# First MoE's last outputs placed among the second MoE's slots, and other places for the second pair's operands

## The chip, the cores and the metric

The kernel runs on one core of a Trainium2 chip. The metric is the device time of one execution in microseconds. Before the change the median of three runs is 922.1 us (922.1, 922.1 and 923.27).

## The reference, cut to what matters

```python
# q, k, v: 4 batches, 8 heads, 576 positions, head size 64
q_s = softmax(q, axis=-1); k_s = softmax(k, axis=2)
kv  = einsum('bhsd,bhse->bhde', k_s, v)
x   = einsum('bhsd,bhde->bhse', q_s, kv)      # as 2304 tokens x 512
# first MoE, d_ff 1536
x = ((x @ w_a) * (x @ w_b)) @ w_out
# second MoE, d_ff 2048
h = x @ w_in
P = a0 + a1*h + a2*h**2 + a3*h**3
Q = 1 + |b0|*|h| + |b1|*h**2
out = (P / (Q + 1e-6)) @ w_out2
```

## The kernel before, in words

Every matmul operand of the two MoEs is split in two float32r halves, a high and a low one, and each product is three matmuls: high x high, high x low, low x high (`mm3`, L446 to L449, and L637 to L639 in `mult`). XH and XL hold the halves of the 2304 tokens of the layer's input, as four chunks of 128 features. The tokens are cut into blocks: blocks 0 to 3 are 512 wide and block 4, the narrow one, is 256 wide. ACC holds the sums of the outputs.

**Order of the work.** The kernel writes down every instruction with an engine, an estimated duration, a rank and its reads and writes (class Plan, L35). `Plan.run` (L65) then plays the program through: of all instructions whose inputs are there it takes the one that can start first, and among equals the one of lower rank. The order that comes out is the order in each engine's queue; the chip keeps it, whatever its own durations are. So ranks and duration estimates decide only the order. DMAs are all issued on SP's queue.

**First MoE.** `step1` (L469) handles one filter group f (128 of the 1536 hidden features) for one block n: the a projection into one PSUM bank, a copy of it by ScalarE (L475), the b projection into a second bank, their product on VectorE (L478), its high half on ScalarE (L481) and low half on VectorE (L482). The output products of the step, `rest` (L485), come after the projections of the next step, and go to the banks Y, four of them. After three filters the four banks are added to ACC (L465, or copied there by L463 the first time). There are four filter groups of three, and 60 steps (n1); in the first three groups the block order is 0, 1, 2, 4, 3, in the last one 0 to 4. The last group of the narrow block is done apart by `last_narrow` (L500): bank 4 holds the a projection in its left and the b projection in its right half, so that each filter's copy (L518), product (L519) and split (L523, L524) stand in a chain with the projections; then come the output products, the addition to ACC (L538) and the split of the result into XH and XL (L540, L541). Its ranks are LAST = 60.3 and on.

**Second MoE.** Its input projection is a Strassen-Winograd form: two 512-wide blocks of tokens, two halves of the features and two filters are treated as 2 x 2 blocks, with 7 products in place of 8. `operands` (L549) makes the seven token operands of one pair of blocks from ACC: `less` (L567) subtracts in ACC, `split` writes the high half by ScalarE (L560) and the low one by POOL (L562) or VectorE (L564). Each operand lies in a place of XH and XL, `place(c, b, r)`: chunks 2c + r, block b, so it overwrites tokens that are not read any more. Pair 0 is blocks 0 and 1, pair 1 blocks 2 and 3, and both pairs use the same seven places (`spots`, L791).

A slot (L648) is one pair of filters j for one pair of blocks: seven operands of the weights are loaded from DRAM (they were put there during the first MoE by the `spill` functions), seven products of six matmuls run through the banks ba, be, bb, bc, with copies and additions between banks (L658, L660, L663, L665), and `value` (L587) works out P/Q of each of the four banks in place: five instructions on ScalarE (L593 to L595, L601, L602), one on POOL (L596) and five on VectorE (L597, L598, L603, L605, L607). With `extra`, the filters of the narrow block are projected too, from the same weights, in a fifth bank. There are 16 slots: 8 for pair 0, all with `extra`, then 8 for pair 1. After every second slot `jobs` (L695) issues the output products of a group of four filters: `whole` (L611) splits the value (ScalarE L619, POOL L620), and each 128 tokens are 4 x 3 matmuls into banks 0 and 1 and an addition to ACC.

Buffers are handed out in rings (class Ring, L234): r_op for the weights' operands, r_w2 for the output weights, r_o for the splits of values, r_free and r_seed for PSUM banks. They reuse places of the first MoE's weights and splits (wa, fa).

## Time and profile before

| what | before |
|---|---|
| median of three runs | 922.1 us |
| the profiled execution's own time | 919.76 us |
| its span, first to last instruction | 917.7 us |
| mean granted clock of TensorE | 0.996 |
| busy: TensorE / VectorE / ScalarE / POOL | 893.9 / 647.5 / 554.1 / 408.9 us |

The profile lists for each engine the busy time, and for idle time what ended it. A matmul's record is longer than its pace, since matmuls are pipelined: the pace is read from the starts. PE is TensorE, PEld its weight loads, DVE VectorE, ACT ScalarE, SP the DMA queue. PEclk is the granted clock as a share of full speed. A wait "PE ps L449 <- POOL wa L620" is idle time of TensorE ahead of a matmul of line 449, ended by an instruction of POOL of line 620. The attention and the first MoE go together until 137 us; the second MoE's first product starts at 513.85 us.

### The profile page before, as it was taken

How to read it: one execution, taken by the hardware profiler on the slowest of the kernel's cores; microseconds unless marked ns; L12 is line 12 of the kernel's file. 1: busy time of each engine (PE TensorE's matmuls, PEld its weight loads, DVE VectorE, ACT ScalarE, POOL GpSimd, SP SyncE). 2: the span in 40 equal slices, each digit the busy share in tenths (PEclk: the TensorE clock that was granted, in tenths of full speed). 3: DMA queues.
4: the chain of work that ended last, by engine and by line, in shares of the span. 5: the costliest groups of instructions: out<-in, count | busy, mean ns of one | idle time of the engine just before them, and what ended most of it. 6: DMA issues, size and time to landing. Idle time of an engine off the chain costs nothing.

```text
span 917.7 us, 13161 instructions
## 1 busy us (share of the span) xinstructions
PE 893.9 (97%) x4577; PEld 737.3 (80%) x4577; DVE 647.5 (71%) x1051; ACT 554.1 (60%) x1046; POOL 408.9 (45%) x369
## 2 busy tenths in 40 slices
PE   7999999999999999999989898999999899999998
PEld 6677778888898888988878777888888688888886
DVE  5799642366666866676784479667879978678883
ACT  5978562454444444444442479888687777887771
POOL 4553320235542354535461145636356764455552
PEclk9999999999999999999999999999999899999999
DMA  7655510236664367645431443152433346363422
GB/s 268 192 196 161 181 30 1 91 116 208 220 216 139 117 221 231 206 141 186 142 112 46 149 150 114 57 185 81 151 126 93 135 141 229 96 194 83 157 69 92
DMA packets 60034, 131.23 MB, mean 143 GB/s; under 512 B 6464, under 2 KB 14656, under 8 KB 59968
## 3 DMA queue, kind: packets, MB, share of 16 engines
q1 hardware_dynamic: 59680, 130.39, 44.3%
q8 instruction: 36, 0.59, 0.3%
q14 instruction: 30, 0.25, 0.1%
q10 hardware_dynamic: 288, 0.00, 0.0%
HBM read 100.49 MB, written 29.88 MB: 142 GB/s over the span
## 4 chain that ended last, share of the span: by engine, by line
PE 89%; DVE 5%; ACT 3%; POOL 2%; issue 1%; DMA 1%; ACTq 0%; POOLq 0%; DVEq 0%
PE ps L447 23%; PE ps L449 23%; PE ps L448 23%; PE ps L637 5%; PE ps L639 5%; PE ps L638 5%; PE ps L428 2%; PE ps L402 1%; PE ps L418 1%; DVE ACC L567 1%; DMA coef<-in_moe_b 1%; DVE ACC L465 1%; PE ps L369 1%; DVE fa L280 0%; POOL fa L319 0%
## 5 line engine op out<-in xcount | busy, mean ns | idle before, releaser
L447 PE MATMUL ps<-wa 128*128 128x512 f32 (+1 forms) x528 | 203.9, 386 | 3.4 <-ACT wa L481 1.4
L449 PE MATMUL ps<-wa 128*128 128x512 f32 (+1 forms) x528 | 201.7, 382 | 3.9 <-POOL wa L620 3.9
L448 PE MATMUL ps<-wa 128*128 128x512 f32 (+1 forms) x528 | 201.6, 382 | 1.0 <-DVE wa L482 1.0
L447 PE MATMUL ps<-XH,wa 128*128 128x512 f32 (+1 forms) x528 | 195.5, 370 | 2.7 <-DVE ps L519 1.1
L449 PE MATMUL ps<-XH,wa 128*128 128x512 f32 (+1 forms) x528 | 190.5, 361 | 0.2 <-POOL wa L290 0.2
L448 PE MATMUL ps<-XL,wa 128*128 128x512 f32 (+1 forms) x528 | 190.4, 361 | 0.0
L596 POOL TENSOR_TENSOR fa<-fa 128x512 f32<-128x512 f32 x72 | 93.8, 1307 | 128.2 <-ACT fa L594 117.4
L620 POOL TENSOR_TENSOR wa<-fa,wa 128x512 fp32r<-128x512 f32 x72 | 93.2, 1311 | 61.7 <-ACT wa L619 48.1
L447 PEld LDWEIGHTS ps<-wa 128*128 128x128 f32 x528 | 99.6, 189 | 25.1 <-ACT wa L619 2.0
L449 PEld LDWEIGHTS ps<-wa 128*128 128x128 f32 x528 | 99.7, 189 | 24.4 <-POOL wa L620 5.5
L447 PEld LDWEIGHTS ps<-XH,wa 128*128 128x128 f32 x528 | 99.7, 189 | 20.2 <-ACT wa L523 1.4
L448 PEld LDWEIGHTS ps<-wa 128*128 128x128 f32 x528 | 99.8, 189 | 20.0 <-DVE wa L482 1.8
L290 POOL TENSOR_TENSOR wa<-fa,wa 128x512 fp32r<-128x512 f32 x36 | 50.3, 1403 | 139.5 <-ACT wa L289 135.2
L449 PEld LDWEIGHTS ps<-XH,wa 128*128 128x128 f32 x528 | 99.6, 189 | 15.9 <-POOL wa L290 0.7
L448 PEld LDWEIGHTS ps<-XL,wa 128*128 128x128 f32 x528 | 99.8, 189 | 14.6
L307 POOL TENSOR_TENSOR fa<-fa 128x256 fp32r<-128x256 f32 x96 | 76.2, 817 | 68.9 <-ACT fa L306 65.9
L465 DVE TENSOR_TENSOR ACC<-ps,ACC 128x512 f32<-128x512 f32 (+1 forms) x110 | 72.2, 670 | 36.1 <-PE ps L449 35.9
L478 DVE TENSOR_TENSOR ps<-ps,fa 128x512 f32<-128x512 f32 (+1 forms) x57 | 37.4, 656 | 84.4 <-PE ps L449 84.2
L481 ACT ACTIVATE wa<-ps 128x512 fp32r<-128x512 f32 (+1 forms) x57 | 32.0, 564 | 88.9 <-DVE ps L478 88.9
L603 DVE SCALAR_TENSOR_TENSOR fa<-fa,coef,ps 128x512 f32<-128x512 f32 x72 | 52.9, 743 | 28.7 <-ACT ps L602 28.4
L279 ACT ACTIVATE fa<-fa 128x512 f32<-128x512 f32 x68 | 45.7, 680 | 30.9 <-DVE fa L277 30.3
L597 DVE TENSOR_TENSOR fa<-fa,ps 128x512 f32<-128x512 f32 x72 | 49.1, 683 | 21.3 <-ACT fa L595 21.1
(113 smaller groups left out, 1652.3 us busy)
## 6 DMA issues: line engine op xcount, KB each, us to landing
wi<-fa SPq DMA_DIRECT2D x64, 256.0 KB, 3.9
wa<-wo SPq DMA_DIRECT2D x32, 512.0 KB, 4.4
wa<-wi SPq DMA_DIRECT2D x60, 256.0 KB, 3.0
fa<-in_moe_w_out SPq DMA_DIRECT2D x28, 512.0 KB, 4.2
fa<-in_moe_w_in SPq DMA_DIRECT2D x16, 512.0 KB, 3.7
wo<-fa SPq DMA_DIRECT2D x32, 256.0 KB, 4.3
XH<-wi SPq DMA_DIRECT2D x30, 256.0 KB, 3.0
XL<-wi SPq DMA_DIRECT2D x30, 256.0 KB, 2.8
```

The costliest lines, as they stand in the source:

```text
L290: pool(W, rank, lambda: nc.gpsimd.tensor_tensor(out=t[:, 1, :], in0=hf, in1=t[:, 0, :].bitcast(F32), op=ALU.subtract), [kr, kw], [kw])
L307: pool(HALF, rank, lambda: nc.gpsimd.tensor_tensor(out=lo, in0=src, in1=hi.bitcast(F32), op=ALU.subtract), [ksrc, kt], [kt])
L447: nc.tensor.matmul(o, lh, rh, start=start, stop=False)
L448: nc.tensor.matmul(o, lh, rl, start=False, stop=False)
L449: nc.tensor.matmul(o, ll, rh, start=False, stop=stop)
L465: dve(n, rank, lambda: nc.vector.tensor_tensor(out=a, in0=ps[bank][:, :n], in1=a, op=ALU.add), [psk(bank), ("accr", o)], [("accr", o)])
L596: pool(n, rank, lambda: G.tensor_tensor(out=w, in0=w, in1=u, op=ALU.mult), [ku, kw], [kw])
L597: dve(n, rank, lambda: V.tensor_tensor(out=z, in0=z, in1=h, op=ALU.mult), [kz, kh], [kz])
L603: dve(n, rank, lambda: V.scalar_tensor_tensor(out=z, in0=z, scalar=coef[:, 0:1], in1=h, op0=ALU.add, op1=ALU.mult), [kz, kh], [kz], ptr=1)
L620: pool(W, rank, lambda: nc.gpsimd.tensor_tensor(out=hl[:, 1, :], in0=z, in1=hl[:, 0, :].bitcast(F32), op=ALU.subtract), [kz, kh], [kh])
L637: T.matmul(ps[bank], wh, xh, start=first, stop=False, skip_group_check=True)
L638: T.matmul(ps[bank], wh, xl, start=False, stop=False, skip_group_check=True)
```

## The change

The narrow block's tokens move out of XH and XL into a tile XN of their own, which begins with 64 unused bytes, and its products' halves start 64 bytes into their buffer as well (SIDE). `last_narrow` goes; in the last filter group the block order is 0, 1, 4, 2, 3, so the narrow block has ordinary steps there. The last three steps (block 3) are only `front`; their output products are `late_jobs`, with ranks among the first two slots. Slots 0 and 1 have no `extra` any more; the two missing ones are done in slots 12 and 13, since pair 1 takes the filters in the order 4 to 7, 0 to 3. The second pair's first operand goes to place (1, 3), the other six each to the place of the operand one earlier. Place (1, 3) held weights before; `wa` has three more buffers and `fa` one. The matmul of L802, which read the negative identity, goes. Ranks, which were written in the calls, come from a table K, and duration estimates of VectorE's instructions with two SBUF inputs (dve3) and of ScalarE (178 in place of 150 after the first MoE) are raised.

```diff
-    NW, NRAW, NHL, NSC = 10, 3, 3, 7
+    NW, NRAW, NHL, NSC, NEW = 10, 3, 3, 7, 3
-    LAST = 60.3
-    LATE, SOON = 0.25, -2.0
+    TURN1, NX, SW0, SW1, OP1 = 4, 2, 2, 3, NF2 // 2 - 1
+    FREE, SEED = (4, 5, 6), (2, 3, 7)
+    K = dict(late=0.004, soon=-2.088, asoon=-2.101, wl=1.191, j0=0.621, j1=1.847, jn=1.96, each=0.208, by=0.383, v1=-0.223, v2=0.25, v3=1.089, v4=0.415, v5=0.458, p1=0.05, px=0.629, op=-0.518, w2=0.507, w2f=1.839, o0=-4.578, o1=-1.102, l0=2.934, l1=2.627, l2=2.373, l3=3.783, last=0.577, nx=-4.91, wn=2.147)
...
-    XH = const.tile([P, NCC, NT], F32R, name="XH")
-    XL = const.tile([P, NCC, NT], F32R, name="XL")
+    NW4 = NT // W * W
+    SIDE = 16
+    XH = const.tile([P, NCC, NW4], F32R, name="XH")
+    XL = const.tile([P, NCC, NW4], F32R, name="XL")
+    XN = const.tile([P, 8 * SIDE + 2 * NCC * (NT - NW4)], F32R, name="XN")
...
+    def dve3(n, rank, fn, reads, writes):
+        plan.add("dve", 150 + n * 1.76, rank, fn, reads, writes, port=True)
...
-            act(w, rank, lambda o=o, px=px: A.activation(XH[:, hp, o:o + w], px[:, 0:w], AF.Copy),
-                [kpx], xk("XH", hp, o, w))
+            for a, e in pieces(o, w):
+                xh = X(0, hp, o + a, e - a)
+                act(e - a, rank, lambda px=px, a=a, e=e, xh=xh: A.activation(xh, px[:, a:e], AF.Copy),
+                    [kpx], xk("XH", hp, o + a, e - a))
...
+    def front(f, n, banks, rank):
...
+        o = SIDE if n == NB - 1 else 0
+        hh, ll = hl[:, 0, o:o + nb], hl[:, 1, o:o + nb]
...
-    def last_narrow(fs, ranks):
...
+    def late_jobs(n, hs, ranks):
+        t0, nb = blocks[n]
+        for m, rank in enumerate(ranks):
+            sl = slice(m * P, (m + 1) * P)
+            bank = m % 2
+            for i, (f, (hh, ll, kh)) in enumerate(hs):
+                w, kw = wtile["o", f]
+                pe(3, nb, rank + 0.01 * i, lambda w=w, sl=sl, bank=bank, hh=hh, ll=ll, i=i: mm3(
+                    ps[bank][:, :nb], w[:, 0, sl], w[:, 1, sl], hh, ll, i == 0, i == len(hs) - 1),
+                    [kw, kh], [psk(bank)], fixed=13)
+            add_acc(NCC * t0 + m * nb, nb, bank, False, rank)
...
+    LASTG = [0, 1, NB - 1, 2, 3]
-             for n in (order if g < NF1 // G1 - 1 else range(NB))]
+             for n in (order if g < NF1 // G1 - 1 else LASTG)]
...
-        if n == NB - 1 and b == NF1:
+        if s >= n1 - G1:
             if f == a:
                 pend()
-                last_narrow(range(a, b), [LAST + 0.1 * i for i in range(b - a)])
                 pend = lambda: None
+            late.append((f, front(f, n, AB if s % 2 == 0 else AT, s)))
...
-    pend()
+    abase[0] = 178
+    late_jobs(NB - 2, late, [n1 + K[f"l{i}"] for i in range(4)])
+    narrow_x(n1 + K["nx"])
...
-    r_op = Ring(wa.cuts([(6 * 2 + i) * W for i in range(2)], OP) + spare + wa.cuts([(7 * 2 + i) * W for i in range(2)], OP))
-    r_w2 = Ring(wt(9, 0, 1, 3, 4))
+    r_op = Ring(wa.cuts([(t * 2 + i) * W for t in (13, 14, 6, 7) for i in range(2)], OP))
+    r_w2 = Ring(wt(0, 1, 3, 4, 9))
...
+    r_o = Ring(ha[2:] + ha[:2], ha[:2] + [((h, l), kh + kl) for (h, kh), (l, kl) in spare])
-    r_free, r_seed = Ring((5, 3, 4)), Ring((6, 7, 2))
+    r_free, r_seed = Ring(FREE), Ring(SEED)
...
-    spots.append(spots[0])
+    spots.append([(1, 3)] + spots[0][:-1])
+    turns = [list(range(NP2)), [(j + TURN1) % NP2 for j in range(NP2)]]
-    operands(0, spots[0], n1 - 3.0, 2)
+    operands(0, spots[0], n1 + K["o0"], SW0)
...
-        extra = js < NP2
-        slot(js, js % NP2, spots[js // NP2], extra)
-        if js == 0:
-            pe(1, W, step2_rank(0, 0.2), lambda: nc.tensor.matmul(ps[2], minus, XH[:, 0, 0:W], start=True, stop=True),
-               xk("XH", 0, 0, W) + [psk(2)], [psk(2)], fixed=13)
-        if js == NP2 - 1:
-            operands(1, spots[1], step2_rank(NP2, -0.5), 3)
+        p, i = divmod(js, NP2)
+        j = turns[p][i]
+        extra = j >= NX if p == 0 else j < NX
+        slot(js, p, j, spots[p], extra)
+        if js == OP1:
+            operands(1, spots[1], step2_rank(NP2, K["o1"]), SW1)
...
-    jobs(2 * (NB // 2) - 1, NF2 // G2 - 1, NS + 0.6, 0.01, (4, 3, 5, 2), 0.6)
+    jobs(2 * (NB // 2) - 1, turns[1][-1] // gp, NS + K["last"], 0.01, False, True, (4, 3, 5, 2), 0.6)
```

## Rows read from the trace of the kernel before

**Rows 1.** The page: busy time, share of the span and instructions of each engine.
```profile
PE 893.9 (97%) x4577; PEld 737.3 (80%) x4577; DVE 647.5 (71%) x1051; ACT 554.1 (60%) x1046; POOL 408.9 (45%) x369
```

**Rows 2.** Windows: stretch, width, busy PE, PEld, DVE, ACT, POOL; clock; DMA share, GB/s.
```profile
137.00:460.00 323.00, 323.00 (x1577) 273.46 (x1576) 203.85 (x349) 138.27 (x271) 127.81 (x142) 1.00 0.50 160
460.00:505.00 45.00, 42.56 (x186) 34.37 (x185) 28.73 (x38) 14.91 (x30) 19.91 (x18) 1.00 0.20 71
505.00:545.00 40.00, 36.83 (x219) 31.86 (x217) 21.35 (x37) 23.54 (x41) 10.61 (x10) 1.00 0.52 162
545.00:570.00 25.00, 21.12 (x98) 16.30 (x98) 22.81 (x36) 22.41 (x38) 12.43 (x10) 1.00 0.33 98
570.00:704.00 134.00, 134.00 (x657) 113.64 (x656) 104.20 (x159) 106.45 (x179) 70.95 (x56) 1.00 0.36 111
704.00:735.00 31.00, 27.74 (x109) 21.23 (x108) 30.33 (x42) 23.87 (x41) 23.76 (x17) 0.89 0.46 154
735.00:880.00 145.00, 145.00 (x642) 120.03 (x641) 114.26 (x173) 114.08 (x192) 72.44 (x58) 1.00 0.45 141
```

**Rows 3.** Waits view, TensorE: total us, times, longest us.
```profile
PE ps L449 <- POOL wa L620: 3.9, 3, 2.6
...
PE ps L447 <- ACT wa L481: 1.4, 1, 1.4
...
PE ps L447 <- DVE ps L519: 1.1, 1, 1.1
...
PE ps L447 <- DVE ACC L538: 0.5, 1, 0.5
```

**Rows 4.** Timeline of TensorE around a wait: start, duration, instruction.
```profile
547.77 0.39 PE L639 MATMUL ps<-XH 128*128 128x512 f32 x1
549.49 0.50 PE L637 MATMUL ps<-XH,XL 128*128 128x512 f32 x1 [1.33 <-DVE ps L663]
549.83 0.39 PE L638 MATMUL ps<-XL 128*128 128x512 f32 x1
```

**Rows 5.** Timeline of TensorE after the longest wait.
```profile
726.47 0.61 PE L449 MATMUL ps<-wa 128*128 128x512 f32 x1 [2.63 <-POOL wa L620]
...
727.30 0.63 PE L448 MATMUL ps<-wa 128*128 128x512 f32 x1
727.72 0.63 PE L449 MATMUL ps<-wa 128*128 128x512 f32 x1
```

**Rows 6.** The page: DMA issues, KB each, median us to landing.
```profile
wa<-wo SPq DMA_DIRECT2D x32, 512.0 KB, 4.4
```

**Rows 7.** Groups by line and form, 570 to 704 us, ScalarE, VectorE, POOL: count, busy, mean ns.
```profile
L594 ACT ACTIVATE fa<-fa,bmag 128x512 f32<-128x512 f32 x25 | 20.1, 817 | 3.8 <-DVE ps L605 3.8
...
L605 DVE SCALAR_TENSOR_TENSOR ps<-fa,qbias,ps 128x512 f32<-128x512 f32 x27 | 20.0, 748 | 0.0
L597 DVE TENSOR_TENSOR fa<-fa,ps 128x512 f32<-128x512 f32 x25 | 17.0, 684 | 4.6 <-ACT fa L595 4.5
L465 DVE TENSOR_TENSOR ACC<-ps,ACC 128x512 f32<-128x512 f32 x16 | 10.9, 689 | 4.9 <-PE ps L449 4.8
...
L596 POOL TENSOR_TENSOR fa<-fa 128x512 f32<-128x512 f32 x25 | 32.3, 1300 | 33.8 <-ACT fa L594 32.7 <-DVE fa L603 1.0
```

**Rows 8.** Groups by line and form, 704 to 735 us, VectorE and POOL.
```profile
L567 DVE TENSOR_TENSOR ACC<-ACC 128x512 f32<-128x512 f32 x8 | 8.7, 1099 | 0.0
...
L562 POOL TENSOR_TENSOR XL<-ACC,XH 128x512 fp32r<-128x512 f32 x8 | 11.0, 1395 | 5.9 <-ACT XH L560 5.9
```

**Rows 9.** The same subtraction in 570 to 704 us.
```profile
L567 DVE TENSOR_TENSOR ACC<-ACC 128x512 f32<-128x512 f32 x1 | 0.7, 684 | 0.0
```

**Rows 10.** The split of attention, 100 to 137 us, ScalarE.
```profile
L431 ACT ACTIVATE XH<-ps 128x288 fp32r<-128x288 f32 x8 | 3.3, 412 | 1.3 <-PE ps L428 0.8
```

**Rows 11.** Timeline of TensorE in a visit to the narrow block.
```profile
259.63 0.28 PE L449 MATMUL ps<-XH,wa 128*128 128x256 f32 x1
259.75 0.28 PE L447 MATMUL ps<-XH,wa 128*128 128x256 f32 x1
```

192 lines of the change are left out of this document (87 added, 105 removed).

## The prediction

> **What bounds the kernel now.** I read the page first. TensorE is busy for 893.9 of the 917.7 us of the span [rows 1], so a change that leaves the products as they are can win only where TensorE stands. Next I read the windows view, cut where TensorE's share falls. From 137 to 460 us, from 570 to 704 and from 735 to 880 TensorE has no idle time at all [rows 2]; VectorE has slack there (114 of 145 us in the last). Between them lie three weak stretches: the end of the first MoE with its narrow block (460 to 545), the first slots of the second MoE (545 to 570), and the change from its first token pair to its second (704 to 735). Their idle is width minus PE: 2.44, 3.17, 3.88 and 3.26 us, together 12.75.
>
> The waits view, from which rows 3 show four, names thirteen waits in these four stretches, from 2.6 us (POOL's low half in L620) down to 0.5 us (the adds of L538) [rows 3]; two lie in 460 to 505, five in 505 to 545, four in 545 to 570, two in 704 to 735. A wait costs more than its idle. In the timeline a dense 512-column matmul starts 0.227 us after the one before; around an idle time of 1.33 us the two starts are 1.72 and 0.34 us apart [rows 4], so 1.60 is lost: 0.27 beyond the idle. Around the wait of 2.63 us the clock falls too: the starts 0.43 us apart [rows 5] are the 1.2 GHz level against 0.227 at 2.4 GHz. From 726.5 to 733.4 us fourteen matmuls go at that pace: 14 x 0.20 = 2.8 us.
>
> The loss that can be won back, by stretch:
> - first MoE's end: 2.44 + 2 x 0.27 = 2.98
> - narrow block: 3.17 + 5 x 0.27 = 4.52
> - first slots: 3.88 + 4 x 0.27 = 4.96
> - change of pair: 3.26 + 2 x 0.27 + 2.8 = 6.60
>
> That is 19.06 us. The profiled execution took 919.76 us, 2.3 under the median of 922.1; I subtract from the median, since none of the terms depends on the offset.
>
> **The narrow block becomes an ordinary step.** Before, L500 runs the last three filters of the narrow block through one bank, in a chain a, copy, b, multiply, split, add; its waits run from 1.1 us for the product of L519 to 0.5 for L538 [rows 3]. After, the block takes the ordinary pairs of banks and stands between blocks 1 and 2, so the next step's projections lie under its chain. The rows for that are 137 to 460, where it is visited as such a step and TensorE is not idle [rows 2]. Ends: 0 and today's 4.52. I take 0.3.
>
> **The last outputs move.** The last three steps (512-wide block 3) become fronts only; their output products, 4 x 3 x 3 = 36 matmuls or 36 x 0.227 = 8.2 us, are issued among slots 0 and 1. So nothing on TensorE waits any more for the L481 and L482 of the last steps, of which L481 gave the 1.4 us in the first stretch [rows 3]. That wait came because VectorE was giving the operands' subtractions (L567) their turns. The subtractions now have rank 55.4 instead of 57 and still stand ahead of the last fronts, but there only the late products wait. Ends: 0 and 2.98. I take 0.5, for block 2's outputs, which still wait for their splits. What the late products hold until then (three split buffers, three weights) is asked for last by the reordered rings, and places 13 to 15 are new; without that cover the first loads would wait some 4.4 us for a landing [rows 6].
>
> **The first slots.** A slot has 42 matmuls, 9.5 us, but four values. A value has five VectorE instructions, 0.684 to 0.748 us, sum 3.6 us [rows 7]; with L663 and L665 at 0.7 a slot asks VectorE for 15.8 us. Until jobs can start, VectorE is the limit. The change moves the extra (narrow) value of slots 0 and 1 to slots 12 and 13 (2 x 3.6 = 7.2 us of VectorE; 735 to 880 has 30 us of slack [rows 2], without which 7.2 would be the price), and gives TensorE 8.2 us of late products where it had 12.9 us of narrow ones. VectorE needs 2 x 15.8 + 4 late additions at 0.69 = 34.4 us for slots 0 and 1, and begins some 5.5 us in (three products and two ScalarE steps, [rows 7]). Slot 2 needs the bank of slot 1's third value, at about 5.5 + 34.4 - 3.6 = 36.3 us; TensorE has work until 9.5 + 8.2 + 9.5 + 4 products (5.4) + narrow extra (2.9) = 35.5. So about 1 us is late, if the late products fall exactly into the gaps; I take 3. The lower end is 0, the upper is worked out below.
>
> **The change of pair.** The second pair's operands are 22 instructions with both inputs in SBUF: on VectorE 8 subtractions and 4 splits, on POOL 10. Here L567 takes 1099 ns and POOL's L562 1395 [rows 8], against 684 for an L567 with POOL free [rows 9]. Before, the first of them overwrites a place that slot 7 still reads, so the whole burst of 12 x 1.1 = 13.2 us on VectorE lands in 700 to 732, where VectorE is busy 30.3 of 31 us [rows 2], and L620 comes late behind POOL's splits. After, the first operand goes to a place that nobody reads any more, and each other one to the place of the product one earlier. Both halves of the first operand and four of the eight subtractions can then run before slot 7: 4 + 1 of 12 VectorE instructions, 5.5 us. The waits to hide are 3.26 us. Ends: 0 and 6.6. I take 2, because the other 17 still crowd one slot.
>
> **Small terms.** The matmul with the negative identity at slot 0 goes: -0.2. A 288-wide split in attention is cut in two for four units: at most one more L431, 0.41 us [rows 10], four times, under a TensorE that is busy; 0, at most 1.6 without cover. Weights are loaded at later ranks on SP's queue, whose DMA share is 0.36 to 0.45 in the slots [rows 2]: 0, at most one landing of 4.4 [rows 6]. The narrow block's own halves (four copies on ScalarE, four subtractions on POOL, 256 wide) are now issued some three steps ahead of slot 0, in 460 to 505, where POOL is busy 19.9 of 45 us and ScalarE 14.9 [rows 2], and first read in slot 2: 0. Larger rings and other cost figures in the planner add no instruction. The second pair's other order of filters is the same work.
>
> **The 64 bytes.** Narrow matmuls start 0.12 us apart [rows 11], 13 ns over their 256 columns at 2.4 GHz; the wide ones, 0.227, are over theirs by the same 13. The trace of before has no shifted one. There are 12 x 2 x 4 x 3 + 12 x 4 x 3 + 8 x 8 x 3 = 624 of them; if the shift took all 13 away it would win 8.0 us; a like loss is not excluded. I take 0, because both widths show the same surplus, so that it does not look like a matter of where the narrow block lies.
>
> The Trainium skill's page "TensorE: Matmul & The Clock Gate" ("Wait — 56ns, not 53.3ns?") gives a warm matmul its columns plus about 2.5 ns; by that the narrow ones could be 10 ns faster, and the sum 6 us lower. The trace does not agree with 2.5 ns for these matmuls.
>
> **Sum.** Left over: 0.3 + 0.5 + 3 + 2 = 5.8. Gain: 19.06 - 5.8 + 0.2 = 13.5. 922.1 - 13.5 = 908.6 us.
>
> **Rivals.**
> *The pair's crowd stays* (chance 0.2): the same 22 instructions still share the port in one slot, so the last stretch keeps 6.6. For it: beside POOL's splits an L567 takes 0.4 us longer [rows 8, 9], and a place alone does not change that. Against it: 5.5 us of burst is released early. Time: 908.6 + 4.6 = 913.2.
>
> The skill's page "SBUF — State Buffer" ("Who interferes with whom") says that of a VectorE instruction with two SBUF inputs and a reading GpSimd one the second blocks fully until the first ends; at 0.684 + 1.3 that would be up to 1.98 us each, 23.8 for the twelve in place of 13.2, and this rival the likelier case. The trace agrees with a contention, but its mean of 1.1 is not a full block.
>
> *Everything hides* (0.12): 1 us left in all. 922.1 - 19.06 + 1 - 0.2 = 903.8.
>
> *The narrow pace improves* (0.05): with the main case 908.6 - 8.0 = 900.6.
>
> *Slots run one after the other* (0.08, the slower side). The place is slots 1 and 2, with three banks of each kind and no jobs yet. If each has to wait for the whole of the one before, TensorE stands 15.8 - 9.5 us plus the latency of one value. That chain is Abs, scale, POOL's product, root, square and two VectorE steps: with at most 0.817 for a ScalarE step, 1.3 for POOL's and 0.7 for VectorE's [rows 7] some 6 to 7 us. So 13 us each, 26 in all, less 8.2 of late products, plus two falls of the clock at 2.8: 23.4 us in place of my 3. Time: 908.6 + 20.4 = 929.0. It decides against the change where the first slots lose over 18 us. Against it: before, with five values a slot, they lost 5.
>
> *Waits only change places* (0.04): losses add up to 19 again, 922.
>
> **How the numbers follow.** Main case 0.51, and 0.2, 0.12, 0.05 on the same side: faster 0.88. A measurement of this kernel tells 0.2%, 1.8 us, from no change: same 0.04. Slower 0.08. The range 900 to 918 takes in the main case with its ends (startup up to 10 us, shift of 8 us), and the first three rivals; left out are the two last.
>
> **What would show it.** Right: the PE windows around the end of the first MoE without idle, no wait on a narrow half; the late products lying singly among slot 0's and 1's; first subtractions of the second pair before slot 7; a clock of 1.00 throughout. Wrong: idle over 5 us in the first 40 us of the slots, POOL's L620 as TensorE's longest wait near the change of pair, or a clock near 0.65 anywhere after 460 us.

## The result, and the profile after

The changed kernel takes 898.93 us (median of four, 898.63 to 899.73) against 922.13 us for the kernel before on the same chip (922.1 to 923.27): ratio 0.9747, 95% interval 0.973 to 0.9764. That is 23.2 us by the medians and 20.8 by the profiled executions (919.76 and 898.94); 13.5 was forecast, and the result lies 1.1 us below the range. The medians of the kernels below are of four to ten executions; one of x1_extra_first took 2067.89 us, its three others 900.83 to 901.56.

The page's busy line answers to [rows 1]: TensorE has lost 8.1 us of busy records and its share has risen from 97 to 99%.

```profile
PE 885.8 (99%) x4576; PEld 734.9 (82%) x4576; DVE 638.1 (71%) x1055; ACT 557.5 (62%) x1050; POOL 404.2 (45%) x369
```

The windows of the changed kernel, with the columns of [rows 2]; the cuts follow its own stretches.

```profile
137.00:460.00 323.00, 323.00 (x1583) 273.06 (x1583) 201.51 (x349) 139.00 (x275) 127.97 (x142) 1.00 0.50 163
460.00:505.00 45.00, 45.00 (x246) 39.14 (x245) 28.33 (x48) 17.84 (x38) 19.71 (x22) 1.00 0.26 84
505.00:520.00 15.00, 15.00 (x68) 12.43 (x67) 5.51 (x8) 7.09 (x12) 2.58 (x2) 1.00 0.64 208
520.00:570.00 50.00, 50.00 (x231) 41.30 (x231) 41.99 (x65) 45.67 (x76) 24.42 (x19) 1.00 0.37 111
570.00:690.00 120.00, 120.00 (x588) 101.61 (x587) 100.94 (x154) 102.69 (x172) 70.42 (x55) 1.00 0.39 122
690.00:735.00 45.00, 45.00 (x200) 37.26 (x199) 39.31 (x61) 35.05 (x59) 27.15 (x22) 1.00 0.50 163
735.00:880.00 145.00, 144.79 (x660) 119.92 (x659) 115.24 (x175) 112.90 (x186) 73.13 (x57) 1.00 0.40 127
```

Busy PE equals the width in every stretch up to 735 us. The four weak stretches of before are full, and the clock, 0.89 around the change of pair before, is 1.00.

TensorE's waits over the whole span of the changed kernel (total us, times, longest us), the three longest of the six that the view lists:

```profile
PE ps L392 <- ACT fa L384: 2.4, 1, 2.4
PE ps L833 <- POOL ident masks.py:199: 1.6, 1, 1.6
PE ps L441 <- POOL ACC L414: 0.9, 2, 0.7
```

All six belong to the start, the attention or the preparation of weights; none lies in one of the four stretches, and no wait of [rows 3] has a successor. To count what that is worth I add up, matmul by matmul, the distance from one start to the next minus the pace of its width, from the first narrow matmul of the second filter group (257.95 us before, 258.48 after) to the last matmul of the kernel, and call the sum the **loss by starts**. Only excesses of over 0.04 us are counted. The stretch shrinks from 655.47 to 634.16 us, so by 21.3. The loss by starts falls from 21.5 to 1.2 us (0.36 of it between 520 and 540 us, 0.75 between 860 and 880); 516 narrow matmuls in that stretch are 1.5 ns faster each, 0.8 us; the matmul with the negative identity was 0.2. 20.3 + 0.8 + 0.2 = 21.3: the account closes. Up to 258 us the changed kernel is 0.5 us later, hence 20.8 for the whole.

The late products, by line and form between 513.5 and 545 us (count, busy us, mean ns, idle before them):

```profile
L474 PE MATMUL ps<-wa 128*128 128x512 f32 x13 | 5.1, 389 | 0.0
```

L475 and L476 have 13 each as well; 36 of the 39 are the late products (the last three belong to the first `jobs`). They lie in packets of 9, 18 and 9, from 522.99, 529.28 and 540.44 us, without idle time: the first two in slot 1, which begins at 521.6, the third in slot 2, which begins at 537.4.

The operands of the second pair, VectorE and POOL, 570 to 690 us, against [rows 8, 9]:

```profile
L579 DVE TENSOR_TENSOR ACC<-ACC 128x512 f32<-128x512 f32 x7 | 4.9, 714 | 0.0
...
L574 POOL TENSOR_TENSOR XL<-ACC,XH 128x512 fp32r<-128x512 f32 x9 | 11.8, 1324 | 6.8 <-ACT XH L572 6.2 <-DVE fa L609 0.7
```

Seven of the eight subtractions are done and nine of POOL's ten splits have begun when the second pair's first slot begins at 690.4 us; the first subtraction starts at 633.95. The subtraction takes 714 ns in the mean, not 1099: six of the seven take 0.68 us and one 0.91.

### The profile page after: what moved, and what is told of

Read it like the earlier page. It is cut to its first block, busy times and chain, and to the rows that moved or that the text cites. A ratio compares the mean times of both kernels' runs of the same rounds, so it can differ in the third digit from the quotient of the medians.

```text
span 897.2 us, 13154 instructions
## 1 busy us (share of the span) xinstructions
PE 885.8 (99%) x4576; PEld 734.9 (82%) x4576; DVE 638.1 (71%) x1055; ACT 557.5 (62%) x1050; POOL 404.2 (45%) x369
## 4 chain that ended last, share of the span: by engine, by line
PE 95%; DVE 2%; ACT 1%; DMA 1%; POOL 0%; issue 0%; ACTq 0%
PE ps L474 25%; PE ps L476 25%; PE ps L475 24%; PE ps L649 6%; PE ps L651 6%; PE ps L650 6%; PE ps L451 2%; PE ps L425 1%; PE ps L441 1%; DMA coef<-in_moe_b 1%; PE ps L392 1%; DVE fa L303 0%; DVE small L411 0%; DVE fa L305 0%; DVE ACC L492 0%
## 5 line engine op out<-in xcount | busy, mean ns | idle before, releaser
L474 PE MATMUL ps<-wa 128*128 128x512 f32 (+1 forms) x520 | 199.5, 384 | 0.2
L476 PE MATMUL ps<-wa 128*128 128x512 f32 (+1 forms) x520 | 197.4, 380 | 0.0
L475 PE MATMUL ps<-wa 128*128 128x512 f32 (+1 forms) x520 | 197.2, 379 | 0.0
L474 PE MATMUL ps<-XH,wa 128*128 128x512 f32 x384 | 154.5, 402 | 0.0
L476 PE MATMUL ps<-XH,wa 128*128 128x512 f32 x384 | 150.0, 391 | 0.2 <-POOL wa L313 0.2
L475 PE MATMUL ps<-XL,wa 128*128 128x512 f32 x384 | 149.6, 390 | 0.0
L474 PEld LDWEIGHTS ps<-wa 128*128 128x128 f32 x520 | 97.6, 188 | 19.9 <-DVE ACC L492 1.4
L476 PEld LDWEIGHTS ps<-wa 128*128 128x128 f32 x520 | 97.6, 188 | 18.8
L313 POOL TENSOR_TENSOR wa<-fa,wa 128x512 fp32r<-128x512 f32 x36 | 50.4, 1406 | 138.9 <-ACT wa L312 130.7
L475 PEld LDWEIGHTS ps<-wa 128*128 128x128 f32 x520 | 97.7, 188 | 18.1
L632 POOL TENSOR_TENSOR wa<-fa,wa 128x512 fp32r<-128x512 f32 x70 | 90.4, 1298 | 40.5 <-ACT wa L631 31.5
L525 ACT ACTIVATE wa<-ps 128x512 fp32r<-128x512 f32 (+1 forms) x60 | 33.3, 554 | 88.9 <-DVE ps L521 88.6
L649 PE MATMUL ps<-XH,wa 128*128 128x512 f32 x224 | 87.4, 390 | 0.0
L651 PE MATMUL ps<-XH,wa 128*128 128x512 f32 x224 | 87.2, 389 | 0.0
L650 PE MATMUL ps<-XL,wa 128*128 128x512 f32 x224 | 87.1, 389 | 0.0
L476 PEld LDWEIGHTS ps<-XH,wa 128*128 128x128 f32 x384 | 72.1, 188 | 16.1 <-POOL wa L313 0.7
L474 PEld LDWEIGHTS ps<-XH,wa 128*128 128x128 f32 x384 | 72.2, 188 | 14.5
L475 PEld LDWEIGHTS ps<-XL,wa 128*128 128x128 f32 x384 | 72.2, 188 | 13.6
```

Of the source, the lines that this page charges most:

```text
L313: pool(W, rank, lambda: nc.gpsimd.tensor_tensor(out=t[:, 1, :], in0=hf, in1=t[:, 0, :].bitcast(F32), op=ALU.subtract), [kr, kw], [kw])
L474: nc.tensor.matmul(o, lh, rh, start=start, stop=False)
L475: nc.tensor.matmul(o, lh, rl, start=False, stop=False)
L476: nc.tensor.matmul(o, ll, rh, start=False, stop=stop)
L632: pool(W, rank, lambda: nc.gpsimd.tensor_tensor(out=hl[1], in0=z, in1=hl[0].bitcast(F32), op=ALU.subtract), [kz, kh], [kh])
L649: T.matmul(ps[bank], wh, xh, start=first, stop=False, skip_group_check=True)
```

## The experiments

Every kernel was compared with the kernel before on the same chip. The sets of runs stand on several chips, where the medians of before differ by 1.6 us, so a difference of 1 or 2 us between two kernels is read from the traces, not from the medians. The last column is the loss by starts of the profiled execution; those of q2, s2 and p1 took 914.35, 909.73 and 909.75 us, more than their medians. No run undoes the larger rings, the other PSUM banks (FREE, SEED), the second pair's other order of filters, or the lower `dynamic_dma_scratch_size`, which the diff sets in `build` and the section on the change does not name.

| kernel | median us | ratio, 95% interval | loss by starts |
|---|---|---|---|
| before | 920.6 to 922.1 | 1 | 21.5 |
| after | 898.93 | 0.9747 (0.973 to 0.9764) | 1.2 |
| s1_old_ranks | 909.65 | 0.9856 (0.9839 to 0.9874) | 10.8 |
| s2_old_costs | 906.2 | 0.983 (0.9806 to 0.9853) | 12.1 |
| s4_old_costs_new_order | 904.76 | 0.9818 (0.9799 to 0.9837) | 8.2 |
| j1_jittered_ranks | 901.92 | 0.9786 (0.9764 to 0.9808) | 4.3 |
| l1_no_late | 905.84 | 0.9834 (0.9817 to 0.985) | 7.8 |
| x1_extra_first | 901.43 | 0.9785 (0.9766 to 0.9805) | 3.6 |
| q2_old_structure_new_order | 910.11 | 0.9887 (0.9861 to 0.9913) | 16.2 |
| p1_same_places | 907.02 | 0.9831 (0.9806 to 0.9856) | 9.2 |
| p2_same_places_new_order | 901.14 | 0.9784 (0.9764 to 0.9805) | 3.7 |
| p3_same_places_new_order2 | 898.22 | 0.975 (0.9734 to 0.9766) | 0.7 |
| n1_narrow_step | 923.34 | 1.0024 (1.0015 to 1.0034) | 24.0 |
| b1_before_new_costs | 927.27 | 1.0063 (1.0048 to 1.0078) | 26.7 |
| h1_no_shift | 900.28 | 0.976 (0.9743 to 0.9777) | 1.3 |
| c3_shift_128 | 900.34 | 0.9771 (0.9755 to 0.9788) | 1.5 |
| c2_pad | 910.32 | 0.9878 (0.9861 to 0.9895) | 2.8 |
| c1_wide_shift | 912.02 | 0.9898 (0.9882 to 0.9915) | 1.2 |
| c5_wide_shift_aligned | 906.81 | 0.9841 (0.9826 to 0.9856) | 1.6 |
| v1_first_ranks | 900.42 | 0.9775 (0.9754 to 0.9795) | 2.3 |

### The order: ranks and estimates

**s1_old_ranks** keeps everything but gives the table K the numbers that the calls of before had (0.5 for the late products, which had none).

```diff
+    K = dict(late=0.25, soon=-2.0, asoon=-2.0, wl=1.0, j0=0.85, j1=1.85, jn=1.85, each=0.25, by=0.5, v1=0.1, v2=0.25, v3=0.3, v4=0.35, v5=0.45, p1=0.05, px=0.4, op=-1.0, w2=0.3, w2f=0.2, o0=-3.0, o1=-0.5, l0=0.5, l1=0.5, l2=0.5, l3=0.5, last=0.6, nx=0.3, wn=0.0)
```

> The changed kernel with the ranks that the kernel before had (late 0.25, soon -2.0, operands at -3.0 and -0.5, jobs at 0.85 and 1.85 and so on; the late products, which had none, at 0.5). Everything else of the change stays. If the structure of the change (late products, narrow block as a step, places) took the waits away, it stays at 898.9 to 902. If the searched order did, the 5.8 us that I had left over for the first slots and the change of pair come back or more: 904 to 910, with idle time of TensorE in the first 40 us of the slots.

It is 10.7 us slower than the changed kernel. The first two lines below are from its waits view, the third from its windows:

```profile
PE ps L474 <- DVE fa L619: 3.4, 1, 3.4
...
PE ps L649 <- ACT ps L670: 1.7, 1, 1.7
```

```profile
520.00:570.00 50.00, 44.55 (x200) 36.76 (x199) 40.08 (x60) 40.41 (x69) 23.72 (x19) 0.97 0.35 106
```

TensorE waits again for VectorE's last step of a value (L619), and 7.6 of 10.8 us of loss lie between 520 and 560 us. The same instructions, in an order that is not fitted to them, lose half of the gain.

**s2_old_costs** takes the raised estimates back, and with them `port=True`, by which the planner lets none of these instructions run beside one of POOL.

```diff
-        plan.add("dve", 150 + n * 1.76, rank, fn, reads, writes, port=True)
+        plan.add("dve", 90 + n * 1.15, rank, fn, reads, writes)
...
-    abase[0] = 178
```

> The changed kernel with the planner's duration estimates of before: 679 ns in place of 1051 for VectorE's instructions with two SBUF inputs, which no longer hold POOL in the plan, and 150 in place of 178 for ScalarE. The ranks are the new ones. If ranks and structure are enough, 898.9 to 901. If the plan has to know these durations, L632 is late again around the change of pair and the time is 902 to 908.

**s4_old_costs_new_order** does the same with ranks found anew, by some thousands of small changes of K, each judged by where the kernel's own planner leaves TensorE without work; all ranks "found anew" below come about in this way.

```diff
+    K = dict(late=-9.209, soon=-12.967, asoon=-11.728, wl=-2.729, j0=2.983, j1=2.244, jn=2.573, each=-1.509, by=0.899, v1=2.133, v2=-1.443, v3=2.52, v4=0.596, v5=-2.691, p1=0.093, px=0.73, op=7.798, w2=6.548, w2f=-10.075, o0=6.788, o1=10.108, l0=2.887, l1=2.859, l2=12.584, l3=11.884, last=4.939, nx=-11.98, wn=-24.827)
```

> The changed kernel with the duration estimates of before and the ranks found anew under them. If a search can make up for wrong durations, 898.5 to 900. If the plan is only as good as its durations, waits stay where VectorE's two-input instructions are many (end of the first MoE, change of pair): 902 to 908.

s2 is 7.3 and s4 5.8 us slower than the changed kernel. Of s4, waits and a window:

```profile
PE ps L475 <- DVE wa L526: 1.9, 3, 0.9
...
PE ps L474 <- ACT wa L525: 1.3, 1, 1.3
```

```profile
460.00:505.00 45.00, 41.83 (x218) 35.75 (x217) 30.49 (x44) 16.60 (x36) 21.66 (x22) 0.96 0.24 83
```

The last steps' halves (L525, L526) are late again: 5.2 us of loss between 460 and 480 us. The timeline of VectorE shows what they wait for:

```profile
463.32 3.55 DVE L579 TENSOR_TENSOR ACC<-ACC 128x512 f32<-128x512 f32 x3
466.80 0.41 DVE L526 TENSOR_TENSOR wa<-ps,wa 128x256 fp32r<-128x256 f32 x1
```

Three of the operands' subtractions take 1.18 us each here and stand in front of the half. The old estimate gives them 90 + 512 x 1.15 = 679 ns, the raised one 150 + 512 x 1.76 = 1051. Without a POOL instruction beside it a subtraction does take 0.68 us (the changed kernel's at 633.95); what the old plan leaves out is the wait for POOL (last section). A search that believes 679 does not take them out of the way, and new ranks win back 1.4 of the 7.3 us, with intervals that overlap. Estimate and port mark were undone together, so the share of each stays open.

**b1_before_new_costs** is the kernel before with the raised estimates and their port mark alone.

```diff
+    def dve3(n, rank, fn, reads, writes):
+        plan.add("dve", 150 + n * 1.76, rank, fn, reads, writes, port=True)
...
+    abase[0] = 178
```

> The kernel before with the changed kernel's duration estimates alone (1051 ns for VectorE's instructions with two SBUF inputs, which hold POOL in the plan, and 178 for ScalarE after the first MoE). If the wrong estimates made the waits at the change of pair and at the end of the first MoE, 6 to 9 us go: 913 to 916. If the structure made them, 920 to 923.

It is slower than before. Window and waits of it:

```profile
735.00:880.00 145.00, 139.23 (x608) 113.31 (x607) 108.95 (x165) 109.71 (x184) 73.19 (x57) 1.00 0.44 140
```

```profile
PE ps L641 <- DVE ps L667: 4.0, 2, 3.2
PE ps L641 <- ACT ps L662: 3.8, 5, 1.1
PE ps L641 <- DVE fa L611: 3.1, 1, 3.1
```

The 3.2 us of loss between 460 and 480 are gone, but a stretch that lost nothing before [rows 2] loses 5.8 us of PE. Under the old ranks the better plan is worth nothing here.

**j1_jittered_ranks** is the control: every rank moved at random by some hundredths.

```diff
+    K = dict(late=0.062, soon=-2.104, asoon=-2.107, wl=1.247, j0=0.593, j1=1.841, jn=1.979, each=0.227, by=0.369, v1=-0.174, v2=0.241, v3=1.125, v4=0.469, v5=0.491, p1=0.087, px=0.571, op=-0.584, w2=0.476, w2f=1.863, o0=-4.503, o1=-1.163, l0=2.949, l1=2.584, l2=2.336, l3=3.769, last=0.612, nx=-4.899, wn=2.206)
```

> The changed kernel with each number of the table K moved by a random amount of some 0.05 (a slot is 2.5), and nothing else: how much does a table lose that is near the searched one, but not it? If the ranks have to be right only roughly, 898.5 to 900. If the searched table is a narrow optimum, waits come back here and there: 901 to 905, and then the single removals have to be read against this.

3.0 us slower, by two waits:

```profile
PE ps L649 <- ACT ps L670: 1.7, 1, 1.7
...
PE ps L649 <- DVE ps L675: 1.5, 1, 1.5
```

So an edit undone without a new search can carry some 3 us that have nothing to do with the edit (one random table was tried), and the sum of the single removals (s1, s2, p1, l1 and x1 are 35.5 us together) can't be the sum of their worths.

### The first slots

**l1_no_late** gives the last three steps their output products at once, as in before.

```diff
-        if s >= n1 - G1:
+        if s >= n1:
...
+    pend()
...
-    late_jobs(NB - 2, late, [n1 + K[f"l{i}"] for i in range(4)])
```

> The changed kernel with the last three steps as ordinary steps: their output products come within the first MoE, none are left for the slots. If the late products fill the first slots' waits, these come back without them: 904 to 910, idle time in the first 40 us of the slots. If the narrow block's new place and the order were enough, 899 to 901.

```profile
PE ps L649 <- DVE fa L619: 4.1, 2, 3.4
...
PE ps L649 <- DVE ps L675: 1.8, 2, 1.6
```

```profile
520.00:570.00 50.00, 44.08 (x203) 35.83 (x202) 40.85 (x62) 43.27 (x72) 21.91 (x17) 1.00 0.39 116
```

6.9 us slower; 7.0 of its 7.8 us of loss lie between 520 and 560 us. The first fence is its waits, the second its window: TensorE has run out of work and waits for the values of slots 0 and 1, as the prediction had it.

**x1_extra_first** leaves the narrow extras in slots 0 to 7.

```diff
-    TURN1, NX, SW0, SW1, OP1 = 4, 2, 2, 3, NF2 // 2 - 1
+    TURN1, NX, SW0, SW1, OP1 = 4, 0, 2, 3, NF2 // 2 - 1
```

> The changed kernel with the narrow block's extra value in slots 0 to 7, as before, and none in slots 12 and 13. If VectorE limits the first slots, its 7.2 us more there make TensorE wait 3 to 7 us: 902 to 906. If it does not, 899 to 900.

2.5 us slower, 2.2 of its loss between 540 and 560. That is no more than j1's 3.0, so that the moved extras are worth anything is not shown by this run alone.

**q2_old_structure_new_order** undoes late products, moved extras and new places together (the edits of l1, x1 and p1) and has its ranks found anew.

```diff
+    K = dict(late=-0.077, soon=-2.884, asoon=-4.725, wl=4.331, j0=0.53, j1=2.491, jn=1.944, each=0.22, by=0.469, v1=-0.172, v2=0.038, v3=1.027, v4=0.559, v5=0.651, p1=-0.017, px=0.343, op=6.665, w2=-5.261, w2f=1.753, o0=-2.471, o1=-1.02, l0=4.494, l1=4.522, l2=7.684, l3=-0.903, last=0.788, nx=6.765, wn=4.679)
```

> The changed kernel with three parts of its structure undone at once (no late products, the extra value in slots 0 to 7, the old places) and the ranks found anew for it. New stay the estimates, the rings, the narrow step and the 64 bytes. If order and estimates made most of the gain, 898.5 to 902. If the structure did, the first slots still lose 6 to 10 us, since VectorE has 10 values there and TensorE nothing to do meanwhile: 905 to 910.

910.1 us: 11.2 above the changed kernel, and 11.5 below before. Its waits and the window:

```profile
PE ps L649 <- DVE fa L619: 3.3, 1, 3.3
PE ps L649 <- DVE ps L675: 2.8, 2, 1.4
...
PE ps L474 <- DMA wa<-wo: 2.1, 1, 2.1
```

```profile
520.00:570.00 50.00, 42.56 (x193) 34.12 (x192) 37.22 (x56) 38.74 (x64) 21.88 (x18) 0.93 0.34 103
```

The order that the search found does not fill the first slots: of 16.2 us lost, 11.6 lie between 520 and 580, and the clock falls to 0.93. Another 3.9, between 760 and 780, follow a late load (the DMA wait), as in p2 below; they belong to this table of ranks. The profiled execution is also 4.2 us above the median. Since the places are worth nothing once the ranks fit (p3 below), late products and moved extras together are what fills the first slots; by q2's 11.2 us, with or without those 3.9, I estimate them at 7 to 11 us. How they share it, no run with a new search shows. The rest is order, estimates, rings, the narrow step and the 64 bytes.

### The change of pair

**p1_same_places** lets the second pair use the places of the first.

```diff
-    spots.append([(1, 3)] + spots[0][:-1])
+    spots.append(spots[0])
```

> The changed kernel with the second pair's operands in the first pair's places, so place (1, 3) is not used by them. If the free place is what spread the burst of subtractions, some of the 6.6 us of that stretch comes back: 902 to 906, with idle time of TensorE between slot 7 and slot 8. If order and estimates did it, 898.9 to 900.

```profile
PE ps L474 <- ACT wa L631: 1.6, 1, 1.6
PE ps L476 <- POOL wa L632: 1.2, 1, 1.2
PE ps L474 <- DVE ACC L492: 1.2, 1, 1.2
```

```profile
690.00:735.00 45.00, 41.02 (x167) 32.43 (x166) 36.19 (x56) 31.34 (x54) 25.63 (x20) 0.92 0.42 136
```

8.1 us slower, and TensorE waits at the change of pair again, three times (first fence), and the clock falls to 0.92 (second). Taken alone this would prove the free place.

**p2_same_places_new_order** and **p3_same_places_new_order2** have the same edit and ranks found anew; p3 keeps the ranks of the loads (op, w2, w2f) as the change has them.

```diff
+    K = dict(late=-0.245, soon=-5.609, asoon=-6.42, wl=1.868, j0=0.937, j1=1.951, jn=-0.999, each=0.289, by=0.278, v1=-0.135, v2=0.544, v3=1.068, v4=0.687, v5=0.958, p1=0.054, px=0.967, op=2.391, w2=7.222, w2f=12.825, o0=-4.841, o1=-1.317, l0=3.088, l1=2.573, l2=1.495, l3=12.639, last=0.547, nx=12.203, wn=-4.403)
```

```diff
+    K = dict(late=-1.377, soon=-4.554, asoon=-3.295, wl=0.523, j0=0.769, j1=1.79, jn=2.317, each=0.254, by=0.429, v1=-0.287, v2=0.817, v3=1.368, v4=1.059, v5=1.204, p1=0.025, px=0.529, op=-0.518, w2=0.507, w2f=1.839, o0=-5.732, o1=-1.016, l0=3.7, l1=2.521, l2=5.351, l3=4.89, last=0.447, nx=-3.352, wn=1.037)
```

> As the run with the second pair's operands in the first pair's places, but with the ranks of the table K found anew for these places (some thousands of small changes tried in the kernel's own planner). If the free place itself is worth the 8 us that its removal cost, they stay: 904 to 908, with waits between slots 7 and 8. If the removal only left a table of ranks that fitted other places, the waits go: 898.5 to 900.

> The second pair's operands in the first pair's places, with ranks found anew as before, but with the three ranks of weight loads (op, w2, w2f) held at the changed kernel's: the first table found for these places let two loads come late. If the free place is worth nothing once the ranks fit, 898.5 to 899.5. If it is worth some of the 8 us, a wait stays at the change of pair and the time is 901 or more.

p2 is 2.2 us above the changed kernel, by two loads that land late (`wa<-wo` 0.9 us and `wa<-wi` 0.5); the waits of the change of pair are gone. p3 has none of either, and takes 898.22 us:

```profile
690.00:735.00 45.00, 45.00 (x200) 37.24 (x200) 38.02 (x59) 30.70 (x53) 23.50 (x19) 1.00 0.47 154
```

Its median is the lowest, though its interval (0.9734 to 0.9766) is that of the change. With ranks that fit, the old places do as well. The operands need not be early either: p3's slot 8 begins at 685.3 us, and five of the eight subtractions still lie in it:

```profile
L579 DVE TENSOR_TENSOR ACC<-ACC 128x512 f32<-128x512 f32 x5 | 3.3, 684 | 0.0
```

That is from 685 to 712 us. TensorE fills the time with 72 matmuls of output products, in packets of 12 or 24 between slot 8's own products, from 686.7 to 706.4 us. What empties the change of pair in p3 is this order; the free place is not needed.

### The narrow block as an ordinary step

**n1_narrow_step** is the kernel before with this part alone.

```diff
+    LASTG = [0, 1, NB - 1, 2, 3]
...
-             for n in (order if g < NF1 // G1 - 1 else range(NB))]
+             for n in (order if g < NF1 // G1 - 1 else LASTG)]
...
-        if n == NB - 1 and b == NF1:
+        if s >= n1:
...
+        act(nb, LAST, lambda a=a, xh=xh: nc.scalar.activation(xh, a, AF.Copy), [("accr", o)], xk("XH", m, t0, nb))
+        pool(nb, LAST, lambda a=a, xh=xh, xl=xl: nc.gpsimd.tensor_tensor(
+            out=xl, in0=a, in1=xh.bitcast(F32), op=ALU.subtract),
+            [("accr", o)] + xk("XH", m, t0, nb), xk("XL", m, t0, nb))
```

> The kernel before with one part of the change: in the last filter group the narrow block is an ordinary step between blocks 1 and 2, and its result is split apart; ranks, estimates, places, rings and addresses are those of before. By my sum this takes away the 4.5 us of the narrow chain: 917.6. If those waits only cover others, so that the first slots lose more where the narrow products no longer lie between them, 920 to 925.

```profile
PE ps L637 <- DVE ps L663: 5.7, 1, 5.7
```

```profile
520.00:570.00 50.00, 42.30 (x195) 34.13 (x194) 35.89 (x54) 36.39 (x59) 15.89 (x13) 0.93 0.39 123
```

The narrow chain's own loss goes (500 to 540 us: 4.7 before, 0.8 here), and the kernel gets 0.24% slower: in the first slots, 540 to 580, the loss rises from 5.5 to 12.5, with one wait of 5.7 us for L663. I take it that the chain had lain beside the operands' subtractions and the start of the slots, and that without it TensorE comes to the same dependence sooner. The ranks are those of before, not found anew, so that the part is worth nothing in any order is not shown.

### The 64 bytes

**h1_no_shift** sets SIDE to 0 and keeps the size of the tile; **c3_shift_128** sets 128 bytes.

```diff
-    SIDE = 16
+    SIDE = 0
...
-    XN = const.tile([P, 8 * SIDE + 2 * NCC * (NT - NW4)], F32R, name="XN")
+    XN = const.tile([P, 128 + 2 * NCC * (NT - NW4)], F32R, name="XN")
```

```diff
-    SIDE = 16
+    SIDE = 32
```

> The changed kernel with SIDE = 0: the narrow block's tokens and its products' halves start at the address without the 64 bytes; the tile keeps its size, so all that lies behind it stays where it is. The trace of after has the narrow matmuls 118.0 ns apart, the one before 119.5. If the 64 bytes do that, they are 119.5 apart again and the time is 624 x 1.5 ns = 0.9 us longer, 899.8. If something else does, the spacing stays at 118 and the time at 898.9.

> The changed kernel with 128 bytes in place of 64 ahead of the narrow tokens and their products' halves; the tile keeps its size. If any odd place helps the narrow matmuls, they stay 118.0 ns apart and the time at 898.9. If 64 bytes are a special distance, they go back to 119.5 ns and 899.8, or beyond.

Two rows of a timeline 20 narrow matmuls apart give the pace. The first and the 21st narrow matmul of the same visit, first in the changed kernel, then in h1:

```profile
258.48 0.28 PE L474 MATMUL ps<-XN,wa 128*128 128x256 f32 x1
...
260.84 0.28 PE L476 MATMUL ps<-XN,wa 128*128 128x256 f32 x1
```

```profile
258.10 0.28 PE L474 MATMUL ps<-XN,wa 128*128 128x256 f32 x1
...
260.49 0.28 PE L476 MATMUL ps<-XN,wa 128*128 128x256 f32 x1
```

2.36 / 20 = 118.0 ns with the shift, 2.39 / 20 = 119.5 without; c3 has 2.39 too. 624 x 1.5 ns = 0.9 us, and the medians of h1 and c3 are both 1.4 above the changed kernel; their intervals overlap its own, so the pace carries this reading.

**c1_wide_shift** lets the wide tokens XH and XL begin 64 bytes into their tiles as well; both tiles grow by 64 bytes, so XL's tokens and all that lies behind are 128 bytes further. **c2_pad** leaves every shift as it is and adds 128 unused bytes behind the narrow tile, which displaces what lies after it (weights, sums, scratch). **c5_wide_shift_aligned** has the 64 bytes of c1 in tiles that are 512 bytes longer: XH's tokens are 64 bytes further, XL's 576, and all that lies behind 1024.

```diff
-    XH = const.tile([P, NCC, NW4], F32R, name="XH")
-    XL = const.tile([P, NCC, NW4], F32R, name="XL")
+    XH, XL = (const.tile([P, SIDE + NCC * NW4], F32R, name=nm)[:, SIDE:].rearrange("p (c t) -> p c t", c=NCC) for nm in ("XH", "XL"))
```

```diff
-    XN = const.tile([P, 8 * SIDE + 2 * NCC * (NT - NW4)], F32R, name="XN")
+    XN = const.tile([P, 10 * SIDE + 2 * NCC * (NT - NW4)], F32R, name="XN")
```

```diff
-    XH = const.tile([P, NCC, NW4], F32R, name="XH")
-    XL = const.tile([P, NCC, NW4], F32R, name="XL")
+    XH, XL = (const.tile([P, 128 + NCC * NW4], F32R, name=nm)[:, SIDE:SIDE + NCC * NW4].rearrange("p (c t) -> p c t", c=NCC) for nm in ("XH", "XL"))
```

> The changed kernel with XH and XL starting 64 bytes on as well, so that the wide blocks' tokens, which 1824 matmuls of 512 columns read as their moving operand, have the shift of the narrow ones. If the shift takes 1.5 ns from every such matmul, they start 225.5 ns apart in place of 227.1 and the time is 2.8 us less, 896.2. If it helps narrow matmuls alone, the spacing and the time stay.

> The changed kernel with 128 unused bytes more behind the narrow block's tile, so that the sums, weights and scratch lie 128 bytes further on, as they did with the wide shift, while XH and XL stay. If the 13 us of the wide shift came from the wide tokens' own start, this stays at 898.9. If they came from what lies behind them, 905 to 912.

> XH and XL start 64 bytes on, and each tile is 512 bytes longer, so that the narrow block's tile, the sums and the weights lie at multiples of 512 bytes as in the changed kernel. If a shift of 64 bytes against the weights makes wide matmuls faster too, 227.1 goes to 225.5 ns and the time to 896. If it makes them slower, as the other wide runs had it, they take 230 ns or more and the time is 904 to 912.

All three are slower than the changed kernel, by 13.1, 11.4 and 7.9 us, and hardly wait more (1.2, 2.8 and 1.6 us of loss against 1.2). Dense wide matmuls, 90 starts apart in the changed kernel and 82 apart in c2:

```profile
584.77 0.40 PE L476 MATMUL ps<-wa 128*128 128x512 f32 x1
...
605.18 0.39 PE L476 MATMUL ps<-wa 128*128 128x512 f32 x1
```

```profile
593.30 0.40 PE L650 MATMUL ps<-XL,wa 128*128 128x512 f32 x1
...
612.29 0.39 PE L476 MATMUL ps<-wa 128*128 128x512 f32 x1
```

20.41 / 90 = 226.8 ns against 18.99 / 82 = 231.6. Over the 2520 wide matmuls after 258 us a difference of 4 ns would be 10 us; c2 lacks 11.4, of which 1.6 are waits. So the gain of the narrow operands does not carry over to wide ones. The starts by kind of operand (mean distance from one start to the next, without waits, after 258 us) say more. Wide matmuls that read tokens take 227.1 ns in the changed kernel, 232.7 in c2 and 230.0 in c5; those with both operands in `wa`, which read no token, 227.2, 228.7 and 230.1. So c5's loss is not one of the tokens' start alone, though only that was meant to move.

### The first 40 us

**v1_first_ranks** has new ranks for the attention's units and the first weights' loads besides (U_RANK, W_RANK, U_DMA, W_DMA), which no part of the change touches, to see whether the start-up can be won too.

```diff
+    K = dict(late=0.543, soon=-1.518, asoon=-2.171, wl=1.093, j0=0.551, j1=1.802, jn=1.622, each=0.188, by=0.561, v1=-0.304, v2=0.226, v3=0.982, v4=0.252, v5=0.881, p1=0.045, px=0.641, op=1.498, w2=3.98, w2f=1.928, o0=-4.958, o1=-0.178, l0=2.94, l1=2.674, l2=2.628, l3=6.7, last=4.709, nx=-6.102, wn=1.131)
```

> The changed kernel with new ranks for the attention's units and the first weights as well as a new table K. TensorE still stands for some 7 us of the first 40 and 0.9 at the end. If the first stretch can be had by order, 897 to 898; if attention's inputs limit it, 898.5 to 900.

900.42 us, nothing won: two late loads of `wa<-wo` (0.6 us) came in, and the start-up stayed as it was.

## Why the prediction was wrong

The direction was right and so were the places: the time came out of the four stretches that the windows named, and from TensorE's waits alone but for 1 us. The sizes were not, and one cause was not. By the account from starts, three terms make up 21.3 - 13.5 = 7.8 us:

- **Left over, 5.8.** This is the step that failed. "Ends: 0 and today's 4.52. I take 0.3", "I take 0.5", "I take 3", "I take 2": measured 0.4 in all (the 0.36 us between 520 and 540), so 5.4 us were missed. The counts of work were sound, but I judged each stretch with an order that I had not seen, and put "larger rings and other cost figures in the planner" among the parts that cost and bring nothing since they add no instruction. Ranks and cost figures set the order. s1 and s4 show what a worse order costs with every instruction in place: 10.7 and 5.8 us. Of the four allowances the 2 us for the change of pair had a reason that failed as well: "the other 17 still crowd one slot".
- **The loss, 19.06.** Idle plus 0.27 us per wait came out low: the starts give 20.6 us for the same stretches (460 to 580 and 700 to 740), 1.6 more. The starts stood in the trace of before and could have been added up in place of an allowance for each wait.
- **The 64 bytes, 0.** "Both widths show the same surplus, so that it does not look like a matter of where the narrow block lies": an argument from two unshifted operands cannot speak about a shifted one. Measured 0.8 us in that stretch.

The remaining 2.4 us by which the medians' gain exceeds that of the profiled executions is the offset of which I wrote that none of the terms depends on it. Before, the median lies 2.4 above the profiled execution; after, it lies on it (898.93 and 898.94); in q2, which waits, the profiled execution is 4.2 above its median. The offset went with the waits. The mean granted clock on record goes the same way: 16 executions of the kernel before at 0.996 took 919.7 to 920.7 us, 23 at 0.993 took 921.5 to 924.1. At which waits it fell in the longer ones is not shown, since only one execution has a profile. Without the 2.4 us the result would have been 901.3, inside the range; the 7.8 us would have been missed all the same.

Point by point:

- **Narrow block as an ordinary step**: its own waits went, as forecast, but in n1 the 4.2 us were not won: they moved into the first slots, which nothing fills there.
- **Late products and moved extras**: right in kind. They fill the first slots; without them neither the order of q2, found anew, nor that of l1 does. The gaps were filled wholly, where I left 3 us. The late products do not lie "singly among slot 0's and 1's", as the signs had it, but in three packets in slots 1 and 2.
- **The change of pair**: the waits went, as forecast, but the cause does not hold. "A place that nobody reads any more" was to release four subtractions before slot 7, and four did start before it (slot 7 begins at 661.6 us); but p3 does without the place. In the changed kernel "the other 17 still crowd one slot" did not happen: seven of eight subtractions were over when slot 8 began. In p3 five of the eight did come in slot 8, and TensorE did not wait for them.
- **Rivals.** *The pair's crowd stays* fell: the last stretch lost nothing. The prediction read the mean of 1.1 us as "not a full block". That was a wrong reading, since the mean mixes two kinds. Of the eight subtractions from 703 to 730 us in the trace of before, three take 0.68 us, with no POOL instruction running when they start; the other five, 0.92 to 1.79 us, start while one runs, and each ends 0.55 us after it. The Trainium skill's page "SBUF — State Buffer" ("Who interferes with whom") lets a VectorE instruction with two SBUF inputs and a reading GpSimd one block each other fully, and the trace agrees (rows in the last section). A block costs what is left of the other instruction, so 1.98 us each would be the most and not the rule, and the price depends on the order again. *Slots run one after the other* fell with the full windows from 505 to 570. *The narrow pace improves* was right in sign and eight times too large. *Everything hides* (0.12) is what happened; with 20.6 for the loss, 0.4 left, 0.8 for the narrow pace and 2.4 for the offset its 903.8 becomes 922.1 - 20.6 + 0.4 - 0.2 - 0.8 - 2.4 = 898.5, and 899.0 with the 0.5 that was lost before 258 us. It deserved more: the views already showed, from 137 to 460 us, that an order exists in which TensorE does not idle for 323 us.

## What to carry to other kernels

In a kernel whose engines follow a planned order, durations in the planner and the tie-breaking ranks are parts of the change like any instruction: a plan that leaves out what blocks an instruction hides a wait from the search (s4), and a better plan under old ranks can be slower (b1). A part undone without a new search says little, as p1 (8.1 us) and p3 (0) show for the same edit: search again, more than once (p2 and p3 are 2.9 us apart), or run a control with slightly moved ranks, here 3 us. Where a stage starts with its slow engine empty, keep work of the stage before as filler for the fast one.

## What the runs showed of the hardware

Where an operand begins changes a matmul's pace, in both directions: 256 columns from a place 64 bytes further take 118.0 in place of 119.5 ns (128 bytes further, 119.5 again), while 512 columns go from 226.8 to 231.6 ns when the weights and sums lie 128 bytes further and the tokens stay (c2). In c5 the matmuls of 256 columns with both operands in `wa`, which lies 1024 bytes further, take 114.9 ns against 118.1, and those of 512 columns 230.1 against 227.2. Whether what counts is the place of an operand by itself or of two against each other stays open.

A VectorE subtraction with both inputs in SBUF and a POOL subtraction block each other for as long as the earlier one runs. From the changed kernel, two of VectorE and one of POOL:

```profile
493.95 0.68 DVE L576 TENSOR_TENSOR XL<-ACC,XH 128x512 fp32r<-128x512 f32 x1
494.55 1.78 DVE L579 TENSOR_TENSOR ACC<-ACC 128x512 f32<-128x512 f32 x1
```

```profile
493.98 1.80 POOL L574 TENSOR_TENSOR XL<-ACC,XH 128x512 fp32r<-128x512 f32 x1 [0.75 <-ACT XH L572]
```

L576 starts first and takes its 0.68 us; POOL's instruction takes 1.80 in place of its usual 1.29; L579 starts while that runs, takes 1.78 in place of 0.68, and ends 0.55 us after it.

The same length of wait does not always cost the clock. A wait of 3.35 us in l1, then one of 3.35 us in s1, in their timelines of TensorE:

```profile
539.15 0.50 PE L649 MATMUL ps<-XH,wa 128*128 128x512 f32 x1 [3.35 <-DVE fa L619]
...
539.72 0.39 PE L651 MATMUL ps<-XH,wa 128*128 128x512 f32 x1
539.95 0.40 PE L649 MATMUL ps<-XH,wa 128*128 128x512 f32 x1
```

```profile
552.45 0.58 PE L474 MATMUL ps<-XN,wa 128*128 128x256 f32 x1 [3.35 <-DVE fa L619]
...
553.05 0.42 PE L476 MATMUL ps<-XN,wa 128*128 128x256 f32 x1
553.26 0.41 PE L474 MATMUL ps<-XN,wa 128*128 128x256 f32 x1
```

In l1 the wide matmuls go on 0.23 us apart, at 2.4 GHz (granted clock 1.00 from 539.1 to 542); in s1 the narrow ones start 0.21 us apart in place of 0.118, the 1.2 GHz level (0.50 from 552.4 to 554).

The Trainium skill's page "TensorE: Matmul & The Clock Gate" ("Wait — 56ns, not 53.3ns?") gives a warm matmul in a back-to-back row its columns plus about 2.5 ns. Here every matmul loads weights of its own, and the surplus over the columns is 13.5 ns at 512 and 12.8 at 256 columns (11.3 shifted); no run here shows 2.5.
